# Seven quarter products for two token blocks of a down projection, and an earlier end of the making of w_out's factors

## The chip, the cores and the metric

The kernel runs on one core of one Trainium2 chip. The metric is the device time of one launch in microseconds; lower is better. Each time given as the kernel's is the median of several runs.

## The reference

Attention with routing feeds a two-layer block. Queries and keys are each assigned to one of 16 centroids of their head; a query sees only keys of its own cluster:

```python
mask = q_assign[:, :, :, None] == k_assign[:, :, None, :]
scores = np.where(mask, scale * np.matmul(q, k.transpose(0, 1, 3, 2)), -1e9)
attn = softmax(scores)                      # 4 batches, 8 heads, 768 tokens, head size 64
x = np.matmul(attn, v)                      # bridged to 3072 tokens x 512
h = x @ w_in                                # 512 -> 2048
out = (h - np.tanh(h)) @ w_out              # 2048 -> 512, float32
```

## The kernel before

**The walk.** Attention goes over 96 steps. A step is one pair of heads, one half of the 768 queries, and two of the six key blocks. In each step TensorE computes the scores of the next step (`begin`, line 501), then the weighted values of the present one (`value`, line 558). Between them ScalarE exponentiates (line 523) and VectorE zeroes keys of other clusters (`select`, line 533), using a row of cluster codes that a DMA on SP's queue spreads over the partitions (`spread`, line 456). GpSimd adds the exponentials up over the key blocks (lines 545 and 549). The exponentials live in two buffers, so a select waits until the GpSimd sum of two steps earlier has been read.

**The fill.** After the two attention groups of a step, TensorE gets pieces of the two-layer block of the batch before: a list of items, each with a cost, dealt out so that the costs spent stay in proportion to the steps gone by. All engines then run in the order in which this code emits their instructions. An item calls `between()` after its matmuls; there the step's other work (selects, transposes, routing, loads) is emitted.

The first batch's second half (384 tokens, three blocks of 128) is the fill of steps 24 to 47. Its up projection is 56 items of cost 0.65 (`half_up_items`): for each of eight indices i, seven products of quarter matrices, 192 columns wide (line 926), by the scheme of Strassen and Winograd. VectorE adds the products into `gs[i]` (line 921), ScalarE takes tanh (line 980), GpSimd subtracts it (line 981). Their factors of w_in come from DRAM (`fetch_factors`, line 857) into three buffers in turn, `w_in[0]`, `w_in[2]`, `w_in[1]`. Its down projection is plain: three blocks, each of four items (`project`, line 748) of cost 3.0. An item is 8 matmuls with a weight tile of 64 columns and 512 columns of w_out; the four items of a block accumulate in one PSUM tile, which ScalarE scales (line 756) and a DMA on GpSimd's queue writes out (line 757).

**PSUM.** All these products, the routing scores (line 377) and the sums (lines 592, 619) take turns in a pool of three tiles, `ps_f`. A product waits until the reader of the third tile back is done.

**Factors of w_out.** In steps 36 to 46 VectorE makes the factors that later batches' down projections use (`down_maker`, line 834, eight instructions), and SP's queue writes them to DRAM as they are made (`keep`, line 817, fourteen transfers of 512 KB). The 22 pieces of this work are dealt over the steps named by `light`; steps with index 1 modulo 6, where the next pair is routed, are left out.

**Step 48.** The next fill begins, the second batch's up projection. VectorE first makes its right factors (`right_factors`, line 892). Its first two sets of w_in factors were fetched by the last two indices of the first batch's up projection, at `fetch_factors(base + i + 2)`.

**SP's queue** issues loads and stores in program order. Each of its transfers signals on one of eight semaphores in turn, and issue waits for the transfer eight earlier to have landed; a transfer that reads what another wrote also waits there for it to land, and what stands behind it waits too.

## Time and profile before

| | |
|---|---|
| median of 3 runs | 947.77 us (946.96 to 949.87) |
| the profiled execution | 946.9 us, of it 944.8 us span |
| granted TensorE clock | 0.998 of full |
| TensorE busy with matmuls | 931.7 us, 6558 records |
| VectorE, ScalarE, GpSimd busy | 593.3, 292.9, 512.4 us |
| steps 24 to 35, with the up items | 193.5 to 272.1 us |
| steps 36 to 47, with the down items | 272.1 to 352.1 us |
| a plain down item, `o`, line 748 | 3.43 us on the chain, 16 records |
| two later products of quarters, `pd`, line 1031 | 6.91 us on the chain, 64 records |

In the profile PE is TensorE's matmuls and PEld its weight loads, DVE is VectorE, ACT ScalarE, POOL GpSimd, SP the queue engine. Every float32 matmul of the program leaves two records. Times of day count from the start of the span. "Busy" of an engine is the union of its instructions; matmuls overlap, so that the mean of one matmul is longer than its share of the time.

### The profile page before, as it was taken

Reading aid. Unit: us, or ns where it says so; the run is one execution under the profiler, and the core shown is the slowest. Engines: PE = TensorE matmul, PEld = TensorE weight load, DVE = VectorE, ACT = ScalarE, POOL = GpSimd, SP = SyncE. Lnnn points to the kernel's source line nnn. Section 1 sums busy time; section 2 is a strip of 40 time slices with the busy share of each in tenths; the row PEclk is TensorE's granted clock in tenths of the full one; section 3 lists DMA queues with packets and bytes.
Section 4 is the critical chain, followed back from the end, with each engine's and each line's share of the span. In section 5 each row is a group of like instructions: output and inputs, shape, how many; then the busy total and the mean of one; then the engine's idle time right before and its main releaser. Section 6 shows DMA issues by size and latency. Waiting matters only on the chain.

```text
span 944.8 us, 16918 instructions
## 1 busy us (share of the span) xinstructions
PE 931.7 (99%) x6558; PEld 464.9 (49%) x6558; DVE 593.3 (63%) x1127; ACT 292.9 (31%) x453; POOL 512.4 (54%) x365
## 2 busy tenths in 40 slices
PE   8999999999999999999999999999999999999997
PEld 5434443345643334444466664444456665445664
DVE  7667687887778688576856568766756447443011
ACT  5586554224332232323322121333231220221000
POOL 0136353456675465777785444877797343657500
PEclk9999999999999999999999999999999999999999
DMA  7785474893745655474674647457434222323331
GB/s 179 223 212 144 126 166 139 222 286 109 176 130 148 160 153 133 137 181 131 193 163 172 160 145 208 119 185 171 132 105 149 99 84 101 118 85 127 108 107 37
DMA packets 168456, 139.92 MB, mean 148 GB/s; under 512 B 118272, under 2 KB 146736, under 8 KB 165680
## 3 DMA queue, kind: packets, MB, share of 16 engines
q1 hardware_dynamic: 158816, 115.65, 45.0%
q0 software_dynamic: 6240, 21.50, 7.0%
q10 hardware_dynamic: 3312, 1.61, 0.6%
q8 instruction: 54, 0.88, 0.4%
q14 instruction: 34, 0.28, 0.1%
HBM read 117.48 MB, written 21.24 MB: 147 GB/s over the span
## 4 chain that ended last, share of the span: by engine, by line
PE 88%; DVE 5%; DMA 3%; ACT 1%; issue 1%; SPq 1%; ACTq 0%; DVEq 0%; POOL 0%; POOLq 0%
PE pu L926 27%; PE pd L1031 22%; PE sc L501 13%; PE av L558 12%; PE o L748 5%; PE h L732 4%; DVE e L533 1%; PE sim L377 1%; PE den L619 1%; DVE den L709 1%; PE warm L303 1%; DMA up_factors<-made 1%; DMA row<-q_codes 1%; DVE made L834 1%; DMA raw<-in_moe_w_in_dram 1%
## 5 line engine op out<-in xcount | busy, mean ns | idle before, releaser
L549 POOL TENSOR_TENSOR sum<-sum,e 128x768 f32<-128x768 f32 x112 | 206.8, 1847 | 93.6 <-DVE e L533 89.2
L533 DVE SCALAR_TENSOR_TENSOR e<-row,code,sc 128x384 f32<-128x384 bf16 x336 | 185.0, 608 | 75.8 <-ACT sc L523 52.0
L1031 PE MATMUL pd<-w_in,G 128*64 128x256 f32 (+1 forms) x1728 | 191.6, 379 | 0.0
L523 ACT ACTIVATE sc<-sc 128x768 f32<-128x768 f32 x168 | 125.8, 790 | 195.6 <-PE sc L501 159.3
L1031 PEld LDWEIGHTS pd<-w_in,G 128*64 128x64 f32 (+1 forms) x1728 | 130.5, 144 | 61.7 <-issue 5.9
L926 PE MATMUL pu<-xT,w_in 128*64 128x384 f32 (+1 forms) x1024 | 159.0, 447 | 0.8 <-PE pu L926 0.4
L501 PE MATMUL sc<-t,t 64*128 64x384 f32 x768 | 149.6, 507 | 1.6 <-ACT e L523 0.8
L558 PE MATMUL av<-e,vals 128*64 128x384 f32 x768 | 144.3, 498 | 0.0
L995 POOL TENSOR_TENSOR G<-G,th 128x768 f32<-128x768 f32 (+1 forms) x51 | 87.2, 1725 | 67.6 <-ACT th L993 67.4
L926 PEld LDWEIGHTS pu<-xT,w_in 128*64 128x64 f32 x1024 | 73.1, 137 | 74.8 <-issue 60.5
L501 PEld LDWEIGHTS sc<-t,t 64*128 64x128 f32 x768 | 66.6, 186 | 75.1 <-issue 37.7
L926 PE MATMUL pu<-diff,w_in 128*64 128x384 f32 x576 | 101.7, 487 | 0.0
L545 POOL TENSOR_TENSOR sum<-e 128x768 f32<-128x768 f32 x28 | 52.7, 1881 | 75.4 <-DVE e L533 60.1
L558 PEld LDWEIGHTS av<-e,vals 128*64 128x64 f32 x768 | 47.5, 136 | 81.1 <-issue 79.1
L993 ACT ACTIVATE th<-G 128x768 f32<-128x768 f32 (+1 forms) x51 | 40.9, 806 | 148.9 <-DVE G L921 148.6
L748 PE MATMUL o<-w_out,g 128*64 128x512 f32 x384 | 85.8, 592 | 0.0
L926 PEld LDWEIGHTS pu<-diff,w_in 128*64 128x64 f32 x576 | 40.8, 137 | 52.0 <-issue 45.2
L921 DVE TENSOR_TENSOR G<-pu,u 128x384 f32<-128x384 f32 x72 | 39.7, 551 | 27.0 <-PE pu L926 27.0
L748 PEld LDWEIGHTS o<-w_out,g 128*64 128x64 f32 x384 | 27.5, 137 | 50.5 <-issue 50.2
L1048 DVE SCALAR_TENSOR_TENSOR c<-pd,w_in 128x256 f32<-128x256 f32 x36 | 15.1, 420 | 48.9 <-PE pd L1031 48.9
L732 PE MATMUL h<-xT,w_in 128*64 128x384 f32 x256 | 42.8, 487 | 0.0
L1048 DVE SCALAR_TENSOR_TENSOR w_in<-pd,w_in 128x256 f32<-128x256 f32 x31 | 13.0, 419 | 43.6 <-PE pd L1031 43.1
(144 smaller groups left out, 874.0 us busy)
## 6 DMA issues: line engine op xcount, KB each, us to landing
w_in<-up_factors SPq DMA_DIRECT2D x32, 896.0 KB
w_in<-down_factors SPq DMA_DIRECT2D x21, 1024.0 KB
raw<-in_moe_w_in_dram POOLq DMA_DIRECT2D x16, 512.0 KB, 4.9
raw<-in_moe_w_out_dram POOLq DMA_DIRECT2D x16, 512.0 KB, 4.9
again<-in_moe_w_in_dram SPq DMA_DIRECT2D x32, 256.0 KB
again<-in_moe_w_out_dram SPq DMA_DIRECT2D x32, 256.0 KB
vals<-in_v_dram SPq DMA_DIRECT2D x32, 192.0 KB
row<-q_codes SPq DMA_DIRECT2D x29, 192.0 KB
```

The source lines that it names most:

```text
L501: nc.tensor.matmul(sc[i][:, h, 0:TB], lhsT=turned[n, 1][r].rearrange("p a n -> p (a n)")[:, j * P : (j + 1) * P], rhs=turned[n, 0][r, half ...
L523: nc.scalar.activation(out=out, in_=sc[i][:, :, 0:TB], func=ACT.Exp, scale=SCALE)
L533: nc.vector.scalar_tensor_tensor(out=e[:, h].rearrange("p (j n) -> p j n", n=P), in0=rows[n, half][:, h], scalar=(codes[n][:, h, 1, j : j ...
L545: nc.gpsimd.tensor_tensor(out=s, in0=pair[0], in1=pair[1], op=ALU.add)
L549: nc.gpsimd.tensor_tensor(out=s, in0=s, in1=pair[i], op=ALU.add)
L558: nc.tensor.matmul(avs[n, half][h * D : h * D + D], lhsT=vals[n][:, h, j], rhs=e[i][:, h], start=(j == 0), stop=(j == NCH - 1),)
L732: nc.tensor.matmul(h[r], lhsT=w_in[i][:, c, o * P : (o + 1) * P][:, r], rhs=xT[c][:, half], start=(c == 0), stop=(c == CD - 1),)
L748: nc.tensor.matmul(acc[sub][r], lhsT=gs[f % HF][:, f // HF, sub * P : (sub + 1) * P][:, r], rhs=w_out[f // FQ][:, f % FQ], start=(f == seq ...
L926: nc.tensor.matmul(ps[r], lhsT=streams[base + i][:, c, k_, r], rhs=right[c], start=(c == 0), stop=(c == CH - 1),)
L993: nc.scalar.activation(out=th, in_=t, func=ACT.Tanh)
L995: nc.gpsimd.tensor_tensor(out=t, in0=t, in1=th, op=ALU.subtract)
L1031: nc.tensor.matmul(out_, lhsT=w, rhs=x, start=(i == 0), stop=(i == HF - 1))
```

## The change

Two of the three token blocks are projected down in seven products of quarters; the third stays plain. The left matrix is cut into two token blocks by two halves of the 2048, the right one, w_out, into 2 by 2 quarters. The order of the items becomes: 56 up items, products 1 and 2, the plain block's four items, products 3, 6, 7, 4, 5, each of cost 3.0, so 11 items in place of 12.

- GpSimd makes the left factors: two additions of 128x128 for each i when its up items are done (`done`), eight subtractions after product 1 and eight after product 2. One of the left factors lies in tiles freed by the first batch's values.
- Products 1 to 3 read w_out's quarters; 6, 7, 4 and 5 read made factors, fetched from DRAM by SP's queue: 6, 7 and 4 in the last of the steps that make factors, 5 when product 7 is emitted.
- VectorE combines the products (seven scaled additions from PSUM of 256 columns, one addition in SBUF), ScalarE copies products 1 and 3. Both blocks are written out after product 5.
- The factors of w_out are made in steps 36 and 38 to 42, four pieces a step.
- The first two w_in factors of the second batch are fetched when products 4 and 5 are emitted, and the turn of the three buffers is shifted by four.

```diff
+            if half == 1:
+                def plain(i: int):
+                    return (3.0, 1, lambda between: project(2, i, between))
+
+                sevenths = half_down_items(gs)
+                return (
+                    half_up_items(gs) + sevenths[:2] + [plain(i) for i in range(NQ4)] + sevenths[2:]
+                )
             ups = [(2.6, 1, lambda between, f=f: up(f, between)) for f in sequence]
-            if half == 1:
-                ups = half_up_items(gs)
...
-                t = w_in[(0, 2, 1)[(n + HF) % 3]].rearrange("p c f -> p (c f)")
+                t = w_in[(0, 2, 1)[(n + HF + (len(EXTRAS) if n >= 0 else 0)) % 3]].rearrange("p c f -> p (c f)")
...
-                    fetch_factors(base + i + 2)
+                    if b or i + 2 < HF:
+                        fetch_factors(base + i + 2)
...
+            def done(i: int):
+                g, c, d = gs[i], slice(0, P), slice(P, 2 * P)
+                nc.gpsimd.tensor_tensor(out=half_left[i], in0=g[:, 0, d], in1=g[:, 1, d], op=ALU.add)
+                nc.gpsimd.tensor_tensor(out=g[:, 0, d], in0=g[:, 0, c], in1=g[:, 0, d], op=ALU.subtract)
+
+            return start_without(up_items(0, -HF, quarter, shrink, done))
+
+        EXTRAS, half_left = (6, 7, 4, 5), []
+        extras = {}
+
+        def fetch_extra(e: int):
+            t = w_in[(0, 2, 1)[(HF + e) % 3]].rearrange("p c f -> p (c f)")[:, 0 : HF * HM]
+            extras[e] = t.rearrange("p (a b) -> p a b", b=HM)
+            nc.sync.dma_start(extras[e], down_factors[SLOT[EXTRAS[e]]])
+
+        def half_down_items(gs):
+            outs = {}
+            u = kept_[:, 2048 - 2 * HM : 2048].rearrange("p (a n) -> p a n", a=2)
+            c, d = slice(0, P), slice(P, 2 * P)
+
+            def product(which: int, between):
...
+                if which in EXTRAS:
+                    e = EXTRAS.index(which)
+                    if e == 1:
+                        fetch_extra(3)
+                    elif e > 1:
+                        fetch_factors(e - 2)
+                ps = ps_f.tile([P, HM], F32, name="hd", tag="f")
+                for i in range(HF):
...
+                    for r in halves:
+                        nc.tensor.matmul(
+                            ps[r], lhsT=left[:, r], rhs=right, start=(i == 0), stop=(i == HF - 1)
+                        )
...
+                between()
+                if which == 1:
+                    nc.scalar.mul(out=u[:, 0], in_=ps, mul=float(words))
+                    for i in range(HF):
+                        nc.gpsimd.tensor_tensor(
+                            out=gs[i][:, 0, c], in0=half_left[i], in1=gs[i][:, 0, c], op=ALU.subtract
+                        )
+                elif which == 2:
+                    outs[0] = restp.tile([P, DM], F32, name="osb", tag="rest")
+                    add(outs[0][:, 0:HM], u[:, 0])
+                    for i in range(HF):
+                        nc.gpsimd.tensor_tensor(
+                            out=gs[i][:, 1, c], in0=gs[i][:, 1, c], in1=gs[i][:, 0, c], op=ALU.subtract
+                        )
...
+                elif which == 5:
+                    add(u[:, 0], u[:, 0])
+                    add(outs[1][:, HM:DM], u[:, 1])
+                    put(1)
+                    nc.vector.tensor_tensor(
+                        out=outs[0][:, HM:DM], in0=outs[0][:, HM:DM], in1=u[:, 0], op=ALU.add
+                    )
+                    put(0)
...
-            light = [i for i in range(max(at, 3 * HALF), 4 * HALF - 1) if i % 6 != 1]
+            light = [i for i in range(max(at, 3 * HALF), 3 * HALF + 7) if i % 6 != 1]
...
                 todo += makers[:share]
+                if at >= 2 * HALF and len(makers) <= share:
+                    todo += [lambda e=e: fetch_extra(e) for e in range(3)]
```

More of the change, by code (lines that the diff above doesn't have):

```diff
@@ L763, in plain_items @@
                 order = [(s, i) for i in range(NQ4) for s in range(2)] + order[2 * NQ4 :]
+            if half == 1:
[5 more added lines that the diff above has]
+                )
             ups = [(2.6, 1, lambda between, f=f: up(f, between)) for f in sequence]
-            if half == 1:
-                ups = half_up_items(gs)
             return ups + [
-                (3.4 if half == 0 else 3.0, 1, lambda between, s=s, i=i: project(s, i, between)) for s, i in order
+                (3.4, 1, lambda between, s=s, i=i: project(s, i, between)) for s, i in order
             ]
@@ L981, in shrink @@
                 nc.gpsimd.tensor_tensor(out=t, in0=t, in1=th, op=ALU.subtract)
-            return start_without(up_items(0, -HF, quarter, shrink, lambda i: None))
+            for i in range(0, HF, HF // 2):
+                t = vp0.tile([P, 2, NCH, D], F32, name="vals").rearrange("p a j d -> p (a j d)")
+                t = t[:, 0 : HF // 2 * P].rearrange("p (i n) -> p i n", n=P)
+                half_left.extend(t[:, a] for a in range(HF // 2))
+            def done(i: int):
+                g, c, d = gs[i], slice(0, P), slice(P, 2 * P)
+                nc.gpsimd.tensor_tensor(out=half_left[i], in0=g[:, 0, d], in1=g[:, 1, d], op=ALU.add)
+                nc.gpsimd.tensor_tensor(out=g[:, 0, d], in0=g[:, 0, c], in1=g[:, 0, d], op=ALU.subtract)
@@ new lines, in half_up_items, with add, put @@
+            return start_without(up_items(0, -HF, quarter, shrink, done))
[10 more added lines that the diff above has]
+            def product(which: int, between):
+                f_, cols = {
+                    1: (0, c), 2: (1, c), 3: (1, c), 4: (1, d), 6: (0, c), 7: (0, d), 5: (None, None)
+                }[which]
+                if which in EXTRAS:
[6 more added lines that the diff above has]
+                for i in range(HF):
+                    left = half_left[i] if f_ is None else gs[i][:, f_, cols]
+                    if which in EXTRAS:
+                        right = extras[e][:, i]
+                    else:
+                        f = i if which == 1 else HF + i
+                        m = HM if which == 3 else 0
+                        right = w_out[f // FQ][:, f % FQ, m : m + HM]
+                    for r in halves:
+                        nc.tensor.matmul(
+                            ps[r], lhsT=left[:, r], rhs=right, start=(i == 0), stop=(i == HF - 1)
+                        )
+                def add(out, y):
+                    nc.vector.scalar_tensor_tensor(
+                        out=out, in0=ps, scalar=float(words), in1=y, op0=ALU.mult, op1=ALU.add
+                    )
+                def put(sub: int):
+                    nc.gpsimd.dma_start(out_r[0, HCH + sub], outs.pop(sub))
+                between()
[12 more added lines that the diff above has]
+                        )
+                elif which == 3:
+                    nc.scalar.mul(out=outs[0][:, HM:DM], in_=ps, mul=float(words))
+                elif which == 6:
+                    add(u[:, 0], u[:, 0])
+                elif which == 7:
+                    add(u[:, 1], u[:, 0])
+                elif which == 4:
+                    outs[1] = restp.tile([P, DM], F32, name="osb", tag="rest")
+                    add(outs[1][:, 0:HM], u[:, 1])
+                elif which == 5:
+                    add(u[:, 0], u[:, 0])
+                    add(outs[1][:, HM:DM], u[:, 1])
+                    put(1)
+                    nc.vector.tensor_tensor(
+                        out=outs[0][:, HM:DM], in0=outs[0][:, HM:DM], in1=u[:, 0], op=ALU.add
+                    )
+                    put(0)
+            return [
+                (3.0, 1, lambda between, which=which: product(which, between))
+                for which in (1, 2, 3) + EXTRAS
+            ]
```

## The prediction

> **What bounds the kernel now.** I read the page's busy times first, then the busy times of two stretches, steps 24 to 35 (up items) and 36 to 47 (down items), then the chain of waits in order of time, and last the timelines of the engines around the two joints that the change touches. The page (TensorE, then the others):
>
> ```profile
> span 944.8 us, 16918 instructions
> ...
> PE 931.7 (99%) x6558; PEld 464.9 (49%) x6558; DVE 593.3 (63%) x1127; ACT 292.9 (31%) x453; POOL 512.4 (54%) x365
> ```
>
> The two stretches; columns: length, then busy time of PE, PEld, DVE, ACT, POOL, the clock, the DMA share and GB/s:
>
> ```profile
> 193.50:272.10 78.60, 76.54 (x692) 46.43 (x690) 58.13 (x132) 30.00 (x54) 52.77 (x37) 1.00 0.63 158
> 272.10:352.10 80.00, 80.00 (x436) 29.41 (x434) 62.45 (x91) 23.23 (x35) 46.09 (x28) 1.00 0.60 161
> ```
>
> In the down stretch TensorE never rests; in the up stretch it rests 2.06 us. So a matmul less is time less, as long as VectorE (62 of 80 us busy), GpSimd (46) and the DMA engines (0.60) keep their distance. The chain of waits gives the prices (start, length, what):
>
> ```profile
> 341.72 3.43 PE o L748 x16
> 345.15 1.49 PE sc L501 x8
> 346.64 1.44 PE av L558 x8
> ...
> 467.02 6.91 PE pd L1031 x64
> ```
>
> A plain item (`o`) costs 3.43 us; two products of quarters in the later batches' form cost 6.91, so 3.455 each. Both have 16 weight tiles of 64 columns times 128 rows per item or product: 8 of 512 columns against 16 of 256, so per column they cost the same.
>
> **What the skill says.** The Trainium skill, "Perfetto Trace Analysis", Identifying the Most-Contended Engine, warns that matmul busy time is no measure of TensorE's headroom; so I price by the chain's pace and not by the 99%, and weight loads at 29 of 80 us show that they don't bind. "DMA: Bandwidth & Descriptors", Queues, rings and completion order: SP's transfers share one ring on each DMA engine, and descriptors are taken in ring order. Then a small transfer issued behind 3 MB starts moving when these are through; no line of this trace shows that by itself. The same page, Anatomy of one DMA, puts about 2 us of fixed cost on a transfer, on the GpSimd path; the trace has 1.4 us from one small SP transfer (328.61) to the next that waits for it (330.04). I use 1.4.
>
> **The change part by part.** The sum is against the profiled execution, 946.9 us.
>
> *TensorE's products.* Eight plain items go, 8 x 3.43 = 27.44 us. Seven products come, 7 x 3.455 = 24.19. The third block is untouched. Gain 3.26. No matmul elsewhere is added.
>
> *The deal of items.* The cost falls from 72.4 to 69.4, so a step's share falls from 3.02 to 2.89. By the rule of the deal, step 24 gets 4 up items in place of 5, and the up items end in step 36, with 3. This matters for the one rest of the up stretch (TensorE's timeline; the bracket is the idle time before and its releaser):
>
> ```profile
> 196.30 2.77 PE L926 MATMUL pu<-xT,w_in 128*64 128x192 f32 x32
> 200.95 0.87 PE L926 MATMUL pu<-w_in,w_in 128*64 128x192 f32 x8 [1.88 <-DVE g L921]
> 201.75 1.56 PE L501 MATMUL sc<-t,t 64*128 64x384 f32 x8
> ```
>
> The fifth item waits for an addition that VectorE reaches only after the right factors and a select, at 200.91 by the chain. After the change the scores of the next step stand there instead. They need the same select (198.44 to 200.63), but in two parts: its first half ends about 199.7, so scores run 199.75 to 201.35, values to 202.8, and the delayed item ends at 203.45. Before, the same work was done at 204.68. Gain 1.2, between 0 (VectorE late again at the next items) and 2.1 (all hiccups of this step gone).
>
> *GpSimd.* No addition of 128x128 is in the trace. Rows of 192 columns take 595 ns and of 384 columns 1002, so about 0.46 us by a line through both; 32 of them are 14.7 us. The sixteen of `done` spread over 80 us where GpSimd has 26 idle. The other sixteen come in two bursts of 3.7 us in steps 38 and 39, beside 5.6 us of sums. Following GpSimd's order, the sum of step 40 ends about 2 us into step 40; the exponential's buffer is wanted again only by the select of the step after. Cost taken 0, cover about 4 us; without it a burst would cost its 3.7, and added work can't gain.
>
> *VectorE's combining.* Seven scaled additions of 0.42 us (the form of line 1048) and one in SBUF, taken at the same price: 3.4 us. Those of products 2, 6, 7 and 4 stand in steps with 1.5 us or more idle: 0. Product 5's three come in step 47, before `right_factors`, where VectorE is the late engine:
>
> ```profile
> 346.12 1.21 DVE L834 TENSOR_TENSOR made<-w_out,made 128x1024 f32<-128x1024 f32 x1
> 347.25 2.18 DVE L533 SCALAR_TENSOR_TENSOR e<-row,code,sc 128x384 f32<-128x384 bf16 x4
> 349.35 1.82 DVE L349 STREAM_TRANSPOSE t<-x 128x768 f32<-128x768 f32 x2
> 351.11 2.53 DVE L709 RECIPROCAL den<-den 128x128 f32<-128x128 f32 x3
> 353.67 0.56 DVE L712 TENSOR_TENSOR xT<-xT,den 128x384 f32<-128x384 f32 x1
> 354.15 1.35 DVE L892 TENSOR_TENSOR diff<-xT 128x384 f32<-128x384 f32 x1
> ...
> 358.95 0.55 DVE L921 TENSOR_TENSOR G<-pu,s 128x384 f32<-128x384 f32 x1
> ```
>
> The last `made` (1.13) leaves, product 4's addition (0.42) takes its place, and 1.6 us come in before 354.15: 1.1 us later from there. Late next is the select that follows at 359.41; it frees the score tiles that TensorE wants from 361.47 on, the first one half way, at about 360.5. Some 1 us of slack stands against 1.1 of delay, for the second half less; I take 0.5 us of stall, between 0 and 1.5.
>
> *Making the factors.* The eight `made` instructions only move; step 36 gets two (with GpSimd beside them 2.07 us each) next to a select and three up items, some 7.4 us of VectorE (2.2 the select, 4.1 these, 1.1 three additions) against 4.9 of TensorE. The select of step 38 then ends 6.6 us into step 37, and TensorE asks for it at 8.6. Cost 0; without that cover, about 2.5 (7.4 less 4.9).
>
> *SP's queue.* Fourteen 512 KB stores move earlier. Four loads of 1 MB are new, 6, 7 and 4 in step 42; the two of w_in's factors (896 KB) move to steps 46 and 47, each 7 us or more before use. What is moved past is the row of step 45. Now it is issued at 316.91 and used at 328.50; its values are multiplied at 333.84:
>
> ```profile
> 316.91 0.58 SPq L456 DMA_DIRECT2D row<-q_codes  x1
> ...
> 328.50 2.12 DVE L533 SCALAR_TENSOR_TENSOR e<-row,code,sc 128x384 f32<-128x384 bf16 x4
> ...
> 333.84 1.51 PE L558 MATMUL av<-e,vals 128*64 128x384 f32 x8
> ```
>
> After, on the same clock: the last factor is made at about 317.9, its store lands near 321.4, and only then the third load is issued, the row behind it at 322. Ahead of the row stand that store, 3 MB and a 256 KB output. The DMA engines moved 361 to 426 GB/s in their three busiest us of a later 1 MB load (448 to 451); at that pace the row lands about 330.5 to 331. TensorE is late only if it lands after 332.1. I take 0.3 us, between 0 and 5. Behind the row the head loads, the sums' return, the fourth load and the codes of step 48 slide too; by the same pace each has 2.5 to 4 us left.
>
> Sum: 3.26 + 1.2 - 0.5 - 0.3 = 3.7 us; the profiled execution would be 943.2. The median shown is 0.9 above its profiled run, so the median goes to 944.1. Against no change a difference of 0.3%, 2.8 us, is about what can be told.
>
> **The rivals.** (1) *The joints eat it*: the up stretch keeps its 2 us rest in another place and step 48 pays 1.5: 3.26 - 1.5 - 0.3, about 946.3, the same. For it: VectorE is busy 58 of 78.6 us there in the order given. Against it: the order of the next items shows no wait that is due later than its matmul.
> (2) *A row or its followers come late*: the pace of the new loads is nearer the stretch's mean with its pauses, 161 GB/s, say 180, than 380. Then 3.5 MB need some 19 us from 320 on, the row lands about 340, step 45 waits 8 us, and the codes of step 48 add perhaps 1: 947.8 - 4.0 + 9, about 953. It decides where the wait eats 4.0 + 2.8, from a landing near 338.9. For it: the windows from 320 to 326, full of head loads, moved only 83 to 124 GB/s. Against it: head loads stand behind the row in the queue, not ahead of it. A milder case, 2 to 4 us of wait, lands in the same band, 946 to 948.
> (3) *It doesn't do what it says*: products of 256 columns cost more when VectorE is the reader of each; at 3.9 us a product TensorE gains 0.1, and 947.2 is left. Against it: in the second batch's down items the same form with the same readers runs at 3.455.
>
> **How the numbers follow.** The forecast as above, 943 to 944.9: 0.56. A bigger gain, no stall and fewer hiccups, 942.2 to 943: 0.06. Rival 1: 0.17. Rival 2 mild: 0.10, full: 0.08. Rival 3: 0.03. Faster by over 0.3%: 0.62; within: 0.30; slower: 0.08. The range 942.2 to 947.8 leaves out the full rival 2 and little else; the likeliest case's own range is 943 to 944.9.
>
> **What would show it.** Right: seven `hd` groups of 3.4 to 3.5 us, 112 instructions; scores and not an up item after the first four up items, with under 1.1 us of rest; down stretch without rest; step 48's first up item at about 350.5 in place of 355.1; a TensorE rest of about 0.5 us before the second scores of the second batch's stretch. Wrong: a wait of the select on the row's DMA in step 44 that reaches TensorE's values, GpSimd sums that the selects wait for in steps 39 to 41, or VectorE waits in front of up items at new places.

## The result and the profile after

The change made the kernel slower by a little: median 951.01 us (949.27 to 953.80, 22 executions) against 948.66 for the kernel before in the same series (945.98 to 951.23, 22 executions). The ratio is 1.0025, 95% interval 1.0016 to 1.0035: 2.4 us lost where 3.7 were forecast as won. The profiled execution took 949.29 us (946.9 before), its span is 947.0.

First the head and the busy times of the page of the changed kernel:

```profile
span 947.0 us, 17160 instructions
...
PE 929.5 (98%) x6654; PEld 471.7 (50%) x6654; DVE 595.8 (63%) x1134; ACT 293.7 (31%) x453; POOL 530.8 (56%) x397
```

TensorE has 2.2 us less to do than before, and the span is 2.2 us longer: the kernel now rests some 4.4 us more. Where, the two stretches tell (length, then busy PE, PEld, DVE, ACT, POOL, the clock, the DMA share, GB/s):

```profile
193.50:272.10 78.60, 76.15 (x672) 45.22 (x670) 59.43 (x132) 30.41 (x54) 58.65 (x50) 1.00 0.59 148
272.10:352.10 80.00, 78.47 (x550) 37.52 (x546) 62.08 (x92) 23.65 (x36) 55.93 (x45) 1.00 0.73 209
```

The down stretch, which had no rest, now has 1.5 us of it, and the DMA engines went from 0.60 to 0.73 there. The rests themselves, from TensorE's timeline (start, length, what, and in the bracket the idle time before and its releaser):

```profile
200.47 1.97 PE L501 MATMUL sc<-t,t 64*128 64x384 f32 x8 [0.99 <-DVE e L533]
...
213.92 1.97 PE L501 MATMUL sc<-t,t 64*128 64x384 f32 x8 [0.30 <-DVE e L533]
...
276.68 1.97 PE L501 MATMUL sc<-t,t 64*128 64x384 f32 x8 [0.30 <-DVE e L533]
...
332.12 1.97 PE L501 MATMUL sc<-t,t 64*128 64x384 f32 x8 [0.96 <-DVE e L533]
...
363.71 1.97 PE L501 MATMUL sc<-t,t 64*128 64x384 f32 x8 [1.59 <-DVE e L533]
```

All are scores (`sc`) that wait for a select of VectorE (`e`, line 533). Such a wait costs more than its bracket: the two score tiles then become free one by one, and the pair takes 1.97 us in place of 1.56. The lines at 332.12 (step 45) and 363.71 (step 49, the second scores of the second batch's stretch) are the expensive ones. What stands behind them is in the chain of waits (start, length, what):

```profile
316.63 4.46 DMA down_factors<-made
...
321.48 9.23 DMA row<-q_codes
...
330.83 1.15 DVE e L533 x2
...
332.12 0.93 PE sc L501 x4
...
340.60 4.66 DMA q_codes<-qc
...
345.28 4.61 DMA row<-q_codes
...
362.60 2.11 DVE e L533 x4
...
364.76 0.92 PE sc L501 x4
```

In the kernel before, this stretch of the chain was TensorE alone. Now it runs through DMA: the row of step 45 takes 9.23 us from issue to landing, the store of the next pair's codes 4.66 (issued at 337.66 and followed by its row 2.0 us later before), the row of step 48 another 4.61. What the late row does to VectorE in steps 47 and 48, its timeline shows (the lines of the kernel before stand in the prediction, with the select at 347.25 and the first right factor at 354.15):

```profile
350.00 2.19 DVE L533 SCALAR_TENSOR_TENSOR e<-row,code,sc 128x384 f32<-128x384 bf16 x4 [2.79 <-DMA row<-q_codes]
...
356.91 0.42 DVE L1041 SCALAR_TENSOR_TENSOR w_in<-hd,w_in 128x256 f32<-128x256 f32 x1
...
358.06 0.54 DVE L898 TENSOR_TENSOR diff<-xT 128x384 f32<-128x384 f32 x1
```

The right factors start 3.9 us later than before; 2.75 of it are the select's, about 1.1 product 5's additions. For the select after them, which TensorE waits for, less is left: it starts 3.1 us later (362.52, before 359.41), of which the additions make 0.36. The first right factor took 1.35 us before, beside a GpSimd multiplication (353.72 to 355.09); now that multiplication has ended (357.86) before it, and it takes 0.54.

In what follows T24, T45 and so on are the starts of the scores that stand in step 24, 45 and so on. Between T24 and the first `pd` matmul lies all that the change touches: 273.38 us before, 275.63 after. That length needs no correction for the start of the kernel, which differs between profiled executions by up to 4.5 us (T24 between 193.5 and 198.0) without having been changed.

### The profile page after: what moved, and what is told of

The parts are those of the page before. It is cut to its first block, busy times and chain, and to the rows that moved or that the text cites. A ratio compares the mean times of both kernels' runs of the same rounds, so it can differ in the third digit from the quotient of the medians.

```text
span 947.0 us, 17160 instructions
## 1 busy us (share of the span) xinstructions
PE 929.5 (98%) x6654; PEld 471.7 (50%) x6654; DVE 595.8 (63%) x1134; ACT 293.7 (31%) x453; POOL 530.8 (56%) x397
## 3 DMA queue, kind: packets, MB, share of 16 engines
q1 hardware_dynamic: 159392, 119.85, 45.9%
## 4 chain that ended last, share of the span: by engine, by line
PE 83%; DVE 7%; DMA 5%; ACT 2%; issue 1%; SPq 1%; ACTq 0%; DVEq 0%
PE pu L932 25%; PE pd L1131 23%; PE sc L501 12%; PE av L558 12%; PE h L732 4%; DMA row<-q_codes 3%; DVE e L533 3%; PE o L748 2%; PE sim L377 1%; PE den L619 1%; DVE den L709 1%; PE hd L1036 1%; DVE made L840 1%; DMA up_factors<-made 1%; DMA raw<-in_moe_w_in_dram 1%
## 5 line engine op out<-in xcount | busy, mean ns | idle before, releaser
L748 PE MATMUL o<-w_out,g 128*64 128x512 f32 x256 | 57.0, 592 | 0.0
L927 DVE TENSOR_TENSOR u<-pu,u 128x384 f32<-128x384 f32 x48 | 26.5, 552 | 18.1 <-PE pu L932 18.0
```

The lines of the kernel that those rows point to most:

```text
L748: nc.tensor.matmul(acc[sub][r], lhsT=gs[f % HF][:, f // HF, sub * P : (sub + 1) * P][:, r], rhs=w_out[f // FQ][:, f % FQ], start=(f == seq ...
L927: nc.vector.tensor_tensor(out=out, in0=x, in1=y, op=ALU.add)
```

## The experiments

All runs at a glance. Lengths are from one profiled execution each, ratios to the kernel before from 6 to 22 executions against 22 to 59 of the kernel before. In the kernel before T24 to T48 is 158.62 and T48 to the first `pd` 114.76; 114.76 means that nothing waits there.

| run | T24 to T48 | T48 to `pd` | ratio to before |
|---|---|---|---|
| changed kernel | 158.45 | 117.18 | 1.0025 (1.0016 to 1.0035) |
| e1 row of step 45 first | 157.76 | 118.21 | 1.0032 (1.0021 to 1.0043) |
| e2 product 5 off VectorE | 157.81 | 119.74 | 1.0041 (1.0027 to 1.0055) |
| e3 old deal | 159.00 | 119.12 | 1.0027 (1.0017 to 1.0038) |
| e4 before, new deal | 160.62 | 114.76 | 1.0001 (0.9988 to 1.0014) |
| e6 row first, fourth load late | 161.75 | 114.77 | 1.0011 (0.9998 to 1.0024) |
| e7 loads from ScalarE | 158.41 | 116.17 | 0.9990 (0.9974 to 1.0005) |
| e8 e7 and old deal | 163.25 | 114.76 | 1.0063 (1.0039 to 1.0086) |
| e9 e8, two loads later | 158.06 | 119.85 | 1.0007 (0.9989 to 1.0025) |
| e10 codes from ScalarE | 157.82 | 114.76 | 0.9989 (0.9980 to 0.9998) |
| e11 e10, one addition less | 158.27 | 114.76 | 0.9985 (0.9974 to 0.9996) |
| e12 e11 and old deal | 158.58 | 114.76 | 1.0001 (0.9989 to 1.0012) |
| e13 e4 again | 160.44 | 114.76 | 1.0001 (0.9987 to 1.0016) |
| e14 e11, fourth load from ScalarE | 158.14 | 116.91 | 1.0012 (1.0001 to 1.0024) |
| e15 before, one item moved | 157.51 | 114.77 | 0.9987 (0.9978 to 0.9995) |

### The first four: row, additions, deal

**e1** moves one transfer of the changed kernel.

```diff
-                    if not masked(*to[:2]):
+                    if not masked(*to[:2]) and to[:2] not in rows:
                         spread(*to[:2])
...
+                    todo.append(lambda: spread(*steps[at + 3][:2]))
                     todo += [lambda e=e: fetch_extra(e) for e in range(3)]
```

> The changed kernel, with one transfer moved: the row of step 45 is issued in step 42 ahead of the three 1 MB loads of extra factors, not behind them in step 43. Theory A (the queue, and a chain from it): the late row costs TensorE some 1.7 us at the scores of step 45, and it also makes the codes, their store and with them the row of step 48 late (VectorE waits 2.79 us for that row), which is most of the 2.4 us lost in step 48. Then this edit wins both: the wait of the select on the row goes, 1.7 us come back before step 48 and 1.5 to 2.4 in it, together 3.2 to 4.0 us: slower than before no more, about 947.3. Rival B (the additions): step 48 is late because product 5's three additions (1.4 us) stand ahead of the right factors; the row is only the 1.7 us. Then 1.7 us come back, about 949.3, and step 48 still shows a wait of TensorE of over 1 us.

The time did not move, and yet half of the theory held. VectorE's timeline of this run:

```profile
327.45 2.12 DVE L533 SCALAR_TENSOR_TENSOR e<-row,code,sc 128x384 f32<-128x384 bf16 x4
...
350.99 2.19 DVE L533 SCALAR_TENSOR_TENSOR e<-row,code,sc 128x384 f32<-128x384 bf16 x4 [5.12 <-DMA row<-q_codes]
```

The select of step 44 no longer waits for its row, T44 to T46 fell from 14.84 to 13.44 us (13.38 before): 1.4 us won. All of it and more was lost at the next row: step 48's landed at 351.0 and not at 350.0, the scores of step 48 waited 1.06 us and those of step 49 again 1.59. So the late first row is not what makes the second one late; the codes were never late (VectorE had them at 336.6 here, at 338.0 in the changed kernel, at 337.6 before). Their store is: SP came to it at 341.5, since it stands behind the return of the sums (the store `back` and the loads of it, `den` and `t`) and the fourth load.

**e2** takes product 5's three instructions from VectorE.

```diff
-                    add(u[:, 0], u[:, 0])
-                    add(outs[1][:, HM:DM], u[:, 1])
+                    t = kept_[:, 2048 - 3 * HM : 2048 - 2 * HM]
+                    nc.scalar.mul(out=t, in_=ps, mul=float(words))
+                    for out, y in ((outs[1][:, HM:DM], u[:, 1]), (u[:, 0], u[:, 0])):
+                        nc.gpsimd.tensor_tensor(out=out, in0=t, in1=y, op=ALU.add)
                     put(1)
-                    nc.vector.tensor_tensor(
+                    nc.gpsimd.tensor_tensor(
```

> The changed kernel, with product 5's combination taken from VectorE: ScalarE scales the PSUM tile into SBUF once and GpSimd makes the three additions. VectorE has 1.4 us less ahead of the right factors in step 48. Rival B (the additions make step 48 late): the 2.4 us of step 48 come back, about 948.6. Theory A (the late row makes it late): the right factors start 1.4 us earlier, but the row still comes at 350.0; of the 2.4 us, 1.0 to 1.5 come back, about 949.8, and the select of step 47 still waits 2.8 us for its row.

Neither came: the stretch from T48 got longer by 2.6 us. VectorE's timeline shows where its right factors (line 898) went:

```profile
359.32 1.36 DVE L898 TENSOR_TENSOR diff<-xT 128x384 f32<-128x384 f32 x1
360.72 0.97 DVE L898 TENSOR_TENSOR diff<-xT,diff 128x384 f32<-128x384 f32 x1
```

They take 0.55 us each in the changed kernel; beside GpSimd's multiplication (358.9 to 360.3) and its three additions (360.2 to 363.5) the first four took 1.36, 0.97, 1.08 and 1.35, together 2.6 us more. The Trainium skill, "SBUF — State Buffer", Who interferes with whom, says that a VectorE instruction with two SBUF inputs contends with a GpSimd instruction that reads SBUF, and that one with a single SBUF input, outside the two-port modes, doesn't. The trace agrees for the first (0.55 us alone, 0.97 to 1.36 here); the second no run here tests by itself. The move put three GpSimd instructions beside the right factors, which have both inputs in SBUF. The run tells nothing for rival B, for it put another delay in the place of the one it took away.

**e3 and e4** change the deal alone, in the changed kernel and in the one before. (The costs of the down items set the share of each step, and with it which up item falls into which step.)

```diff
-                    return (3.0, 1, lambda between: project(2, i, between))
+                    return (36 / 11, 1, lambda between: project(2, i, between))
...
-                (3.0, 1, lambda between, which=which: product(which, between))
+                (36 / 11, 1, lambda between, which=which: product(which, between))
```

> The changed kernel, with the costs of its eleven down items set to 36/11 in place of 3.0, so that the sum is 72.4 as before and the up items fall into the steps as before (five in step 24, the last ones in step 35). Theory C (the deal): the up stretch got longer because in steps with four up items TensorE comes to the scores sooner than VectorE's select and waits for the two score tiles one by one (1.97 us against 1.56); then 1.3 to 1.7 us come back, about 949.5, and the split scores at 213.9, 219.6 and 252.8 go. My prediction had it the other way: the old deal should cost 1.2 us, 952.2. Rival D (GpSimd): the sixteen additions on GpSimd slow the up stretch, whatever the deal; then nothing comes back, 951.0.

```diff
-                (3.4 if half == 0 else 3.0, 1, lambda between, s=s, i=i: project(s, i, between)) for s, i in order
+                (3.4 if half == 0 else 2.75, 1, lambda between, s=s, i=i: project(s, i, between)) for s, i in order
```

> The kernel before, with the costs of its twelve down items at 2.75 in place of 3.0, so that the up items fall into the steps as in the changed kernel; no product, addition or transfer is changed. Theory C (the deal): 1.3 to 1.7 us slower than before, all of it in steps 24 to 36, with the scores split where a step has four up items. The prediction's term: 1.2 us faster. Rival D (GpSimd's additions do it): no difference to before beyond 0.3 us.

In the traces theory C holds, and its loss comes out the same to a tenth of a microsecond in every kernel with the new deal. Steps 24 and 25 take 14.8 us on average with the old deal (14.60 to 15.00 in five traces) and 14.15 with the new one (13.75 to 14.73 in ten). But from T26 to T38 the new deal loses 2.3 us, 76.2 us for one 3.43 us item less, against 77.33 before, always at the same places: split scores in steps 27, 33 and 37, and small waits of up items. In e4, which has no addition on GpSimd, the loss is the same, so it isn't GpSimd's (rival D). In the old deal GpSimd's additions cost 0.5 us, in step 35 (7.63 us against 7.14). In e3 the gain was eaten twice: eleven items over twelve steps leave step 41 without one, where the scores wait (steps 41 and 42 took 0.9 us more than two ordinary ones less an item), and TensorE came earlier to the late rows, 1.84 us of rest in step 45 and 1.59 in step 49.

The times don't follow the trace for e4: 2.0 us lost in the trace, 0.1 in the times with an interval of 1.3 to either side. I return to this at e13.

e3 showed something else, in two windows of three microseconds around step 49 (columns as above):

```profile
363.00:366.00 3.00, 1.67 (x8) 0.60 (x8) 3.00 (x7) 0.79 (x1) 1.71 (x1) 0.93 1.15 215
366.00:369.00 3.00, 3.00 (x11) 1.00 (x10) 0.12 (x1) 0.80 (x2) 1.90 (x2) 0.51 0.29 31
```

After the same rest of 1.59 us as in the changed kernel, TensorE's granted clock was 0.51 for about three microseconds; scores and values took 4.9 us in place of 3.2. The changed kernel's profile has 1.00 there. The Trainium skill, "TensorE: Matmul & The Clock Gate", Part 1: The HAM clock gate, says that the clock is halved after an idle window of about 3.4 us, and that the windows run free of the kernel. The 0.51 agrees with the half, the length does not: TensorE rested 1.59 us here and was busy for 2.56 of the three us before these windows, so the measurement decides. The price here is 1.6 us on top of the rest.

### Order on the queue, or bandwidth

**e6** keeps e1's edit and issues the fourth load at product 4, behind the codes' store and the row of step 48.

```diff
-                    if e == 1:
+                    if e == 2:
                         fetch_extra(3)
-                    elif e > 1:
+                    if e > 1:
```

> The kernel with the row of step 45 ahead of the three loads, and beside that the fourth 1 MB load moved behind the codes' store and the row of step 48 (issued at product 4 in place of product 7). In the run with the first row alone moved, TensorE's rest at the scores of step 45 was gone, but the row of step 48 still landed at 351: the codes' store stood right behind the fourth load and took 4.76 us to land (before about 2), the row after it 4.58. Theory A, first form (order on the one queue: a small transfer behind a 1 MB load waits for it): the store lands in about 2 us and the row in about 3, the select of step 47 runs at about 347, the scores of step 48 don't wait, and step 48's second scores wait under 0.6 us: 2.5 to 3.5 us faster than the changed kernel, ratio to before about 0.999 to 1.000. Theory A, second form (SP's queue is held up by the head loads and the return of the sums, which wait behind the three loads): the codes' store itself is still issued at about 341, 3 to 4 us later than before, and the row of step 48 lands at 347 to 349; half of the gain, 1 to 2 us.

The second form: the codes' store was still issued only at 340.81, but landed in 2.09 us, and the row landed at 347.8. Nothing waited in step 48 or 49, but step 48 also began 4.7 us later, so this doesn't show that the row was in time. The load that gave way paid, as the chain of waits shows:

```profile
343.40 6.96 DMA w_in<-down_factors
...
350.41 5.36 PE hd L1036 x32
```

Product 5 waited for its factors until 350.4 and then ran at a reduced clock (0.69 and 0.74 in the two windows of three us from 350) for part of its 5.36 us: step 47 took 11.74 us in place of 7.01.

**e7** issues the four loads from ScalarE's queue.

```diff
-            nc.sync.dma_start(extras[e], down_factors[SLOT[EXTRAS[e]]])
+            nc.scalar.dma_start(extras[e], down_factors[SLOT[EXTRAS[e]]])
```

> The changed kernel with its four 1 MB loads issued from ScalarE's queue in place of SP's; nothing else is changed. If order on SP's queue is what makes the rows late (theory A), the row of step 45 is issued at about 317.5 and lands before 325, the head loads and the sums' return no longer wait for the loads to be issued, the codes' store and the row of step 48 come near their old times, and both rests of TensorE (0.96 and split scores at step 45; 1.59 in step 48) go or shrink to under 0.5: 3 to 4 us faster than the changed kernel, ratio to before about 0.999. If it is the bandwidth of the DMA engines, whichever queue issues the loads, the row of step 45 still lands after 329 and step 48's row after 349, and the time stays that of the changed kernel, ratio about 1.0025.

The row of step 45 was in time (the select at 329.0), the stretch from T48 lost 1.4 us against before and not 2.4, and the ratio came to 0.999 (0.9 us under before, between 2.5 under and 0.5 over; the one profiled execution is 1.2 us over, a difference that stays unexplained like that of e4). But what stands behind the row on SP hardly gained: SP's issue of the head loads lasted until 335.1 (before: 326.2), the codes' store went at 340.71 and the row of step 48 landed at 349.1. The loads left the queue, not the engines. The Trainium skill says so: "DMA: Bandwidth & Descriptors", Issuing engines are not separate DMA queues, has the transfers of all issuing engines run on the same sixteen DMA engines and interleave. One of the head loads took SP 7.8 us to issue (322.72 to 330.54), though its wait for the transfer eight ahead had ended when it began. ScalarE's exponentials stood behind the loads, which waited for the factors' stores; that cost TensorE 0.75 us in step 44.

**e8 and e9** add the old deal, and e9 issues the third and fourth load later, at products 6 and 7.

```diff
-                    if e == 1:
-                        fetch_extra(3)
-                    elif e > 1:
+                    if e < 2:
+                        fetch_extra(e + 2)
+                    else:
...
-                    todo += [lambda e=e: fetch_extra(e) for e in range(3)]
+                    todo += [lambda e=e: fetch_extra(e) for e in range(2)]
```

> The same, and the up items dealt as before (costs of 36/11). In the run with the old deal alone, steps 24 to 36 took 79.04 us against 78.59 before and against 78.17 plus three missing up items (1.95) before in the changed kernel's 77.56: the deal is worth 1 to 1.5 us in the trace, though the timing of the two deal runs did not show it clearly. If both hold, the whole products' gain of 3.26 stays less 0.5 for GpSimd's additions and 0.3 to 1 in step 48: ratio to before 0.997 to 0.9985, steps 24 to 48 in 155.5 to 156.5 us. If the deal does nothing in the time, it is as fast as the run with the loads on ScalarE's queue alone.

> The same again, with the third and fourth loads issued later, one at product 6 and one at product 7, so that only 2 MB and not 3 MB come at once in step 42. If the DMA engines' bandwidth in steps 43 to 45 still delays the head loads and with them the sums' return and the codes, this gives another 0.3 to 1 us over the run with three loads at once; if only the order on the queue mattered, nothing.

Neither came as expected. In e8 TensorE reached step 44 earlier, ScalarE was held by the loads, and the scores rested 5.18 us. In e9 the loads at 330.3 and 333.2 ran into the return of the sums: the 6 KB store `back`, issued by SP at 331.9, landed only at about 341.3 (1.4 us in the kernel before, 2.2 in e1), and with it everything behind it. So a transfer needn't be behind a load in the same queue to be late beside it. Against e8, e9 is 0.1 us shorter in the trace and 5 us faster in the times, where its executions go from 945.2 to 954.6: one trace says little of its mean.

### The codes by themselves

**e10** leaves the loads alone and takes the two small transfers off SP's queue; e1's edit is in it too.

```diff
-            nc.sync.dma_start(kept.rearrange("c (g t) -> g c t", t=BL), t)
+            queue = nc.scalar if n == 2 * HP else nc.sync
+            queue.dma_start(kept.rearrange("c (g t) -> g c t", t=BL), t)
...
+            queue = nc.scalar if (n, half) == (2 * HP, 0) else nc.sync
-            nc.sync.dma_start(
+            queue.dma_start(
                 t, q_codes[n][half].rearrange("j h n -> (j h n)").unsqueeze(0).to_broadcast([P, 2 * TB])
```

> The changed kernel with three small transfers moved and no large one: the row of step 45 ahead of the three loads on SP's queue (as in the first run), and the codes' store of step 45 and the row of step 48 issued by ScalarE in place of SP. In all runs so far SP reached that store only at 341 to 344, though the codes were there at 337 to 338, because the return of the sums stands in front of it and waits behind the loads; the row of step 48 then landed at 347.8 to 351.1. Theory A2 (SP's queue in order is the cause: it holds the codes back): the store goes at about 337.8, the row at about 340 to 341, it lands before 346; no scores wait at step 45 or step 48, steps 24 to 48 take 156.5 to 157 us, and the second scores of step 48 wait 0.3 to 1.1 us for product 5's additions alone: 2 to 3.5 us faster than the changed kernel, ratio to before 0.998 to 1.000. Rival B (product 5's additions): step 48 stays 2.4 us longer than before, ratio to before about 1.001.

ScalarE's timeline, then TensorE's:

```profile
337.08 1.09 ACTq L437 DMA_DIRECT2D q_codes<-qc  x1
339.18 0.36 ACTq L458 DMA_DIRECT2D row<-q_codes  x1
```

```profile
348.73 3.67 PE L1038 MATMUL hd<-w_in,vals 128*64 128x256 f32 x32 [0.56 <-DMA w_in<-down_factors]
...
361.72 1.56 PE L503 MATMUL sc<-t,t 64*128 64x384 f32 x8
```

The store left at 337.1 with the codes just made, the row at 339.2, and the select of step 47 ran at 346.4. Step 48's extra length is gone to the hundredth (114.76), with product 5's three additions in their old place on VectorE: the right factors start 2.15 us after T48, 2.06 before. That settles rival B: with the row in time the additions cost nothing. (T48 is 0.8 us late here, but e8, where nothing was late from step 45 on, has the additions and 114.76 too.) Against the changed kernel this is 3.05 us less in the trace, and 3.4 in the times (0.9989 against 1.0025). What was left is the 0.56 us that product 5 waits for its factors, 0.8 with what follows. The chain of waits shows where that comes from:

```profile
339.18 3.53 DMA row<-q_codes
...
342.72 0.44 SPq L684
...
343.27 5.42 DMA w_in<-down_factors
...
348.73 3.45 PE hd L1038 x29
```

Line 684 is a `t<-back`, which doesn't read that row. But the row, on ScalarE's queue, is the transfer eight ahead of it: the eight semaphores go round over both queues, and SP stood still for 2.4 us. The fourth load behind it was issued at 343.27 (339.98 in the changed kernel).

**e11** takes one of the three instructions away as well: GpSimd adds product 6's sum to the first block at product 4.

```diff
+                    nc.gpsimd.tensor_tensor(
+                        out=outs[0][:, HM:DM], in0=outs[0][:, HM:DM], in1=u[:, 0], op=ALU.add
+                    )
                 elif which == 5:
-                    add(u[:, 0], u[:, 0])
                     add(outs[1][:, HM:DM], u[:, 1])
                     put(1)
-                    nc.vector.tensor_tensor(
-                        out=outs[0][:, HM:DM], in0=outs[0][:, HM:DM], in1=u[:, 0], op=ALU.add
-                    )
+                    add(outs[0][:, HM:DM], outs[0][:, HM:DM])
```

> The same, and of product 5's three instructions on VectorE one is taken away: GpSimd adds product 6's sum to the first block's right half at product 4, where VectorE is idle, and VectorE's two remaining additions read the PSUM tile directly. 0.47 us less of VectorE stands ahead of the right factors of step 48. If what is left in step 48 is the additions (by my sum a stall grows with VectorE's delay one for one once the slack of 1 us is gone), 0.3 to 0.5 us come back in step 48; if a row or anything else on the DMA engines is late, nothing.

In step 48 there was nothing left to win, and nothing came; the ratio, 0.9985, can't be told from e10's. Product 5 waited 1.00 us for its load.

**e12** adds the old deal once more.

> The same again with the up items dealt as before (36/11). In the traces so far the deal is worth this: over six runs with the new deal steps 24 and 25 take 14.2 us on average against 14.75 over four with the old, but from step 26 to the scores of step 38 the new deal loses 2.3 us by scores that wait in two parts. If small transfers no longer wait, TensorE gets that net 1.7 us, less what the step without a down item (step 41) costs, 0.8: steps 24 to 48 in 155.5 to 156.5 us, ratio to before 0.997 to 0.999. If being earlier only makes the DMA engines late (as in the two old-deal runs before), the rows of steps 45 and 48 are waited for again, and the ratio is above 1.000.

Neither branch as written: no row was waited for. Up to T38 the old deal gained 0.9 us on e11 (a product counted at 3.45), and lost 1.1 again by T47, 0.9 of it in steps 41 and 42 as in e3. TensorE was no earlier at product 5, which waited 1.06 us for its load, and step 47 took 8.32. In the times it is the same as before (1.0001).

**e13** is e4 once more.

> The kernel before with the new deal, a second time, because trace and times disagreed: the profiled execution lost 2.0 us in steps 24 to 48, the timed ones 0.1 with an interval of 1.3 to either side. If the trace is right, ratio 1.001 to 1.002; if the deal is worth nothing in the mean of executions, within 0.0005 of 1, and steps 24 to 48 in this profile under 159.5 us.

Again the trace lost 1.8 us, step by step as e4, and again the times show nothing. The mean clock is 0.9984 and 0.9985 in these two against 0.9975 over 151 executions of the kernel before, which would be worth 0.9 us; why it should be higher, no run shows. What the deal costs in the mean of executions stays open; by the two intervals it is no more than 1.5 us.

**e15** moves one item of the kernel before, the fifth, from step 24 to step 25, the one place that the prediction had priced.

```diff
                 ups = half_up_items(gs)
+                ups[4:6] = [(0.9, *ups[4][1:]), (0.4, *ups[5][1:])]
```

> The kernel before with one up item, the fifth, moved from step 24 to step 25; all others stay in their steps. This is the term of the prediction by itself (1.2 us gained, between 0 and 2.1). From six traces with the new deal I expect 0.6 us in steps 24 and 25 (14.1 to 14.2 against 14.78) and the same lengths as before from step 26 on, none of the split scores. In the time there may be more: the granted clock is on average 0.9984 to 0.9985 in the two runs of the kernel before with the new deal and 0.9975 in its own 151 executions; if that comes from the rest of 1.9 us in step 24, this kernel too has a mean clock above 0.998 and a ratio of 0.998 to 0.999. If not, 0.9993.

TensorE's timeline at the scores of step 25, which in the kernel before stand behind a 1.88 us rest of the fifth item:

```profile
202.71 1.96 PE L501 MATMUL sc<-t,t 64*128 64x384 f32 x8 [0.53 <-DVE e L533]
```

Steps 24 and 25 took 13.69 us against 14.78, all steps after them what they took before, to 0.02: 1.1 us won in the trace, and 1.2 in the times (0.9987, so between 0.5 and 2.1). The predicted step was right in kind. Its size is less sure: the wait in step 25 goes from 0.53 us here to 1.57 in eleven traces with the same items in steps 24 and 25, and the ten others gained 0.63 on average. The mean clock is 0.9980, between that of e4 and e13 and that of the kernel before.

**e14** goes back to e11 and issues the fourth load from ScalarE, behind the row.

```diff
-                    if e == 1:
+                    if e == 2:
                         fetch_extra(3)
...
+            queue = nc.scalar if e == 3 else nc.sync
-            nc.sync.dma_start(extras[e], down_factors[SLOT[EXTRAS[e]]])
+            queue.dma_start(extras[e], down_factors[SLOT[EXTRAS[e]]])
```

> The run with the codes and the row of step 48 from ScalarE and one addition less, and beside that the fourth 1 MB load from ScalarE too, behind that row (at about 341 in place of 343.3 to 347.3 from SP, where it stands behind the return of the sums). In the two runs before it, the scores of step 48 came 0.8 and 1.2 us late because product 5 waited for that load. If that was the last wait left in steps 37 to 48, these steps take 73.8 to 74.0 us and nothing waits in step 48: steps 24 to 48 in 156.7 to 157.2 us, 1.5 us less than before and 4 less than the changed kernel, ratio to before 0.9975 to 0.9985. If the load now delays the return of the sums or the values, as it did when it was issued at 333, another wait of about 1 us takes its place and the ratio stays at 0.9985 to 0.999.

The second branch, and worse than it (1.0012). ScalarE issued the load at 338.87, some 4.4 us earlier than SP in e10, and it landed no earlier. TensorE's timeline, then VectorE's:

```profile
348.19 3.67 PE L1039 MATMUL hd<-w_in,vals 128*64 128x256 f32 x32 [1.11 <-DMA w_in<-down_factors]
```

```profile
348.77 0.56 DVE L696 TENSOR_TENSOR xT<-xT,t 128x384 f32<-128x384 f32 x1 [3.29 <-DMA t<-back]
```

The load took 9.3 us in place of 5.4, and now the return of the sums (`t<-back`) came 3.2 us later than in e10 and VectorE's select behind it, so that TensorE rested again before the scores of step 49. In both runs SP issued a `t<-back` only when ScalarE's row had landed (342.6 here, 342.7 in e10); from there VectorE had it after 6.1 us here and 2.9 in e10. The row, with the load right behind it, took 4.5 us (3.5 in e10) and was still in time, so what freed it in e10 was the order and not the absent load. The order decides who is late; that someone is late here seems to be up to the engines, which from 340 to 352 were busy to 0.76 to 0.97 at 229 to 288 GB/s.

## Why the prediction was wrong, step by step

The sum of the prediction against the changed kernel's own profile, T24 to the first `pd`:

| step of the sum | predicted us | measured us |
|---|---|---|
| products of quarters for plain items | -3.26 | -3.3 (3.45 a product on the chain, 3.43 an item) |
| deal, steps 24 and 25 | -1.2 | -0.63, mean of ten traces and in the changed kernel (e15: -1.09) |
| deal, steps 26 to 37 | not priced | +2.3 |
| row of step 45 | +0.3 | +1.4 to 1.5 |
| step 48 and its scores | +0.5 | +2.42 |
| sum | -3.7 | +2.25 |

*The products were right.* The chain of waits of the changed kernel has a product beside a plain item:

```profile
287.26 3.45 PE hd L1036 x32
...
293.64 3.43 PE o L748 x16
```

Seven of these in place of eight of those, as priced; rival 3 is out.

*The deal failed as a step.* I read the one rest that the old deal had and priced its removal, right in kind (1.1 us in e15's trace, 0.63 on average). That the new share of 2.89 puts the whole chain of items elsewhere, and that a step with four up items ends before VectorE's select wherever VectorE has routing or sums to do, I did not follow step by step; I took "no wait that is due later than its matmul", seen in the next items, for the whole stretch. It is rival 1's first half, with 2.3 us in place of its 2. The times of e4 and e13 leave open how much of this the mean of executions sees.

*The row of step 45 failed in size.* "The row lands about 330.5 to 331", from the volume ahead and a pace of 361 to 426 GB/s: it landed at 330.7. The step that failed is the next one, "TensorE is late only if it lands after 332.1": it held the row against the values of step 45, but the scores of step 45 come first and need the two tiles that the select reads. The select takes 2.2 us for two tiles, and TensorE wanted the first at 331.2 and the second 0.8 us later. It cost the wait of 0.96 and the split of 0.41.

*"By the same pace each has 2.5 to 4 us left" is the step that failed worst.* For what stands behind the row on SP's queue I used the pace of bytes alone. What it left out shows in SP's issues, before and after:

```profile
317.53 6.40 SPq L341 DMA_DIRECT2D x<-in_q_dram  x4
...
328.61 0.34 SPq L661 DMA_DIRECT2D back<-each  x1
330.04 1.11 SPq L682 DMA_DIRECT2D den<-back  x2
```

```profile
322.03 8.29 SPq L341 DMA_DIRECT2D x<-in_q_dram  x4
...
333.02 0.57 SPq L661 DMA_DIRECT2D back<-each  x1
337.48 1.11 SPq L682 DMA_DIRECT2D den<-back  x2
```

The sums' store `back` was issued 4.4 us later and landed 7.4 us later (just before `den<-back`). The head loads start 4.5 us later, as forecast, take 1.9 us longer to issue for the first four and 0.3 for the rest, and `back` itself takes 4.4 us and not 1.4; 2.4 us are covered, which SP spent waiting for VectorE before. So the return had 2.4 us to give against 4.5, and two times grew, by 2.2 and 3.0 us, which a pace of bytes doesn't show. The eight semaphores don't explain the longer issue: the transfers eight ahead of the two slow head loads (3.5 and 2.8 us) had landed by 321.1. What holds an issue open, no run shows. The codes' store stood behind the return of the sums, 2.6 us after its codes were ready, with the fourth load right in front of it. e10 shows this as cause: the two small transfers taken off the queue, nothing waits in step 48.

*VectorE's additions were not the cause.* The prediction took 0.5 us for them and named VectorE as the late engine of step 48. Its sum for them is off, too: three additions at its 0.42 are 1.26 and not 1.6, which with the `made` that leaves (1.13 against 0.42) gives a delay of 0.55 and not 1.1; measured at the next select it is 0.36. VectorE was late because the select before them was; in e10 they stand where they stood and cost nothing. The right answer to the sign of step 48 (a rest before the second scores of the second batch) came from the wrong reason, and with 2.42 in place of 0.5: luck.

*GpSimd at zero* held for the path, within the 0.5 us seen in step 35 with the old deal. A burst of eight took 4.34 and 5.32 us and not 3.7; the single addition, estimated at 0.46, took 0.45 to 0.46.

*The chances.* Rival 2 named the right mechanism, the row and its followers, and missed how far the followers reach: it priced the codes of step 48 at "perhaps 1". Its mild form joined to rival 1's first half is what happened, and I had weighed each as if the other gave back the rest of the gain. Both could come at once, as nothing in the profile excluded one when the other holds.

*What is left of the gain.* With the small transfers in time (e10, e11) the changed kernel is faster than before by 0.11 and 0.15%, intervals 0.02 to 0.20 and 0.04 to 0.26. Of the 3.26 us, the trace of e10 keeps 0.8: 1.7 go to the deal and 0.8 to product 5's load. A kernel that keeps all of it would have to fetch less in steps 42 to 47, which was not tried.

## What to carry to other kernels

When loads are added to a queue in program order, follow each small transfer behind them to its own issue, counting how long the issues ahead of it take and which landings it must wait for, and not only the bytes ahead: here a 192 KB row, a 6 KB store and an 8 KB store of codes turned 4 MB of well-hidden loads into two rests of TensorE. Moving transfers to another queue changes who is late, and leaves them among the same eight semaphores. It won for the two small ones (e10) and, with this deal, for the four large ones (e7); it lost in e8 and gave nothing for the fourth load (e14). And where costs set a deal, a changed cost is a change of every step: compare the whole order of both deals with what the other engines have to do in each step, not the place with the largest rest.

## What was unexpected of the hardware

- Two score tiles that become free one after the other make the pair take 1.97 us in place of 1.56, beside the wait itself, in every trace where scores waited for a select at full clock.
- A rest of 1.6 us can halve the granted clock for some three microseconds (0.51 in e3, 0.74 and 0.69 in the two windows after the rest in e2, where it is part of the 2.6 us), or leave it at 1.00 (changed kernel, e1, e14): 1.6 us more in e3, and what decides it no run shows.
- A 1 MB load took 5.4 us when issued at 343.3 (e10) and 9.3 when issued at 338.9 (e14) in the same neighbourhood, and a 6 KB store took 1.4 us (before), 2.2 (e1), 4.4 (changed kernel) or over 9 (e9) depending on what moved beside it, on the same queue or not.
- A load of 96 KB kept SP for 3.5 us in its issue (changed kernel), 5.6 (e10) or 7.8 (e7), with the transfer eight ahead already landed; before, the slowest took 4.2.
- GpSimd instructions in SBUF stretched VectorE's 0.55 us subtractions to 0.97 to 1.36 us.
